# A statically scheduled attention + gated-FFN kernel: wider spacing of score visits, new latencies in the scheduler, and a different split of buffer memory

## The chip, the cores and the metric

One core of one Trainium2 chip. The metric is the device time of one execution in microseconds (us), median of several executions. The profile's span is from the first to the last instruction, here about 1.8 us shorter than the time. TensorE is called PE, VectorE DVE, ScalarE ACT, GpSimd POOL, SyncE SP, as in the profile.

## The reference, cut to what matters

```python
B, S, D, F = 1, 2048, 576, 4608;  H = 32; Dh = 18; W = 256          # bf16
xn = layernorm(x)
q, k, v = split_heads(xn @ wqkv)                                      # 32 heads of 18
p  = softmax(where(0 <= i - j < W, q k^T * Dh**-0.5, -1e9))           # sliding window
s  = concat_heads(p @ v) @ wo
g  = silu((sigmoid(xn @ w_gate) * (xn @ w_up)) @ w_down)
out = x + s * g
```

## The kernel before

The program is one long list of operations (`Op`), each with an engine, an estimated duration and what it depends on. A list scheduler plays the operations through in estimated time and fixes the order on each engine; then code is emitted with semaphore waits. So the constants below don't change what is computed. They change the order.

The sequence is cut into four chunks of 512 rows. For a chunk PE computes the projections of Q, K and V, the scores (in "score visits", short groups of matmuls whose PSUM result ScalarE's exp reads: 5 for each of 8 head groups in 4 chunks, 160 in all), the PV products (16 blocks), the output projection, 36 gate/up tiles and the down projections. Attention of the next chunk runs between the gate/up tiles of this one.

A matmul has 64 rows. Two of them, on the upper and the lower half of the array, run at the same time as a pair (in this kernel's trace 3793 such starts, of some 4150 pairs, are 3 to 4 ns apart). A gate/up tile is 5 pairs, then 4 pairs with the halves swapped. The second part adds to the PSUM banks of the first, so it waits for the first part's semaphore: a "turn" (with nothing in between, the second part starts about 228 ns later than it could). Other matmuls placed between the two parts hide that wait.

```python
NWS = 3            # gate/up weight buffers
NQD = 1            # staging buffers between the Q/K projection and the q/k slots
NFIN = 2           # also the number of tanh buffers of the output stage
NWARM = 36
SPACE_NS = 1100.0  # least distance of two score visits
...
# Pool.pick: when a PSUM unit is free again
free.append((max(now, max(r.end for r in h.rel) + 90.0), self.units.index(u), u))
...
# warm-up matmuls: fillers, taken while PE has nothing else, dropped at the first gate/up tile
w = op("PE", 432 if i < 9 else 216, f_warm, f"warm:{i}", deps=[z], prio=4, acq=None if i else h, odeps=[w])
...
# the output stage: tanh -> t; t *= y; t *= s_attn (the attention branch); x += t
th = op("ACT", act_ns(w), lambda e: f_th(e, 0, 2), f"fth:{nm}", deps=[f2, dt_], prio=0)
q1 = op("DVE", ..., f"fq1:{nm}", deps=[th, f2], prio=0)
q2 = op("DVE", ..., f"fq2:{nm}", deps=[q1, self.op_s[sb]], prio=2)
h.release(q1)                       # PSUM is free after q1 ...
self.r_th.release(st, q3)           # ... the tanh buffer only after the attention branch came
...
# schedule(): candidates of PE
st = max(free[e], ready_t[o.cidx])
if e == "PE" and o.name.startswith("sc"):
    st = max(st, last_sc + SPACE_NS)
...
k = (st + o.prio * self.PRIO_NS, o.cidx)
...
# schedule(): latency from one operation to its successor
lat = (250.0 if o.eng == "PE" and o in s_.deps else 20.0) if s_.eng == o.eng else (200.0 if o.eng == "PE" else 90.0)
if s_.eng == "PE" and o.eng != "PE":
    lat += 600.0 if o.lane is not None else 100.0
```

The softmax here doesn't subtract the row's maximum and nothing guards it: scores larger than these inputs give would overflow.

Of the kernel before, what the change touches and what calls it, by code (L numbers as in the profile page):

```python
# [8 lines left out]
D = 576  # L9
# [12 lines left out]
FG = 4  # L22
NFG = NFT // FG
WG = 2
NWS = 3
EPS = 1e-5
SM_SCALE = float(DH) ** -0.5

# [22 lines left out]
NXR = 2  # L51
NXN = 2
NST = 3
NQD = 1
NFIN = 2
NTAIL = 96
NWARM = 36
PARTS = (((0, 1), (1, 2), (2, 4)), ((0, 1), (1, 2), (2, 4)), ((0, 2), (2, 4)))
# [5 lines left out]
FLIP_ISSUE_NS = 1280.0  # L64
FLIP_SLACK_NS = 2700.0
SHARE_NS = 300.0
SPACE_NS = 1100.0
DMA_BYTES_PER_NS = 280.0
DMA_QUEUE_NS = 2400.0

# [59 lines left out]
class Pool:  # L130
# [11 lines left out]
    def pick(self, n, now, barred=()):  # L142
        free = []
        for u in self.units:
            if u in barred:
                continue
            h = self.last[u]
            if h is None:
                free.append((0.0, self.units.index(u), u))
            elif h.rel and all(r.idx >= 0 for r in h.rel):  # L150
                free.append((max(now, max(r.end for r in h.rel) + 90.0), self.units.index(u), u))
        if len(free) < n:
            return None
        free.sort()
        got = free[:n]
        return max(g[0] for g in got), sorted(g[2] for g in got)
# [70 lines left out]
class Builder:  # L227
# [38 lines left out]
    def alloc_memory(self):  # L266
        nc = self.nc
        bf16, f32 = dt.bfloat16, dt.float32
        cur = [(nc.sbuf_base + 63) // 64 * 64]
        top = nc.sbuf_top  # L270

        def size(shape, dtp):
            n = 1
            for s_ in shape[1:]:
                n *= s_
            return n * mybir.dt.size(dtp)

        def seq(name, shape, dtp=bf16, align=32):
            off = (cur[0] + align - 1) // align * align
            cur[0] = off + size(shape, dtp)  # L280
            assert cur[0] <= top, f"out of SBUF at {name}: {cur[0]} > {top}"
            return nc.alloc_sbuf_tensor_at(name, list(shape), dtp, offset=off), off

        self.xnT, _ = seq("xnT", [P, 2, KB, NT])
        self.wd_sb, _ = seq("wd_sb", [P, NFT, D])
        self.hT, _ = seq("hT", [P, NFT, NT])
        self.wgs, _ = seq("wgs", [P, NWS, KB - 1, 2, WG * P])
        self.wgr, _ = seq("wgr", [P, F])
        self.tring, _ = seq("tring", [P, 2, NT])
        self.v_aug, _ = seq("v_aug", [P, NVS * VSZ])  # L290
        self.qk, _ = seq("qk", [P, NQS, 2, NT])
        self.kprev, _ = seq("kprev", [P, NHG, NT // 2])
        self.kx, _ = seq("kx", [P, NKX, 12, 2, SW])
        self.expr, zex = seq("expr", [P, NEX, 2, NT])
        self.x0 = nc.alloc_sbuf_tensor_at("x0", [P, BPC, D], bf16, offset=zex)
        assert size([P, BPC, D], bf16) <= size([P, NEX, 2, NT], bf16)
        self.ot1, _ = seq("ot1", [P, 1, NT], f32)
        self.o2, _ = seq("o2", [P, 1, NT])
        self.o2T, _ = seq("o2T", [P, 2, NT])
        self.oT, _ = seq("oT", [P, KB, NT])  # L300
        self.s_attn, _ = seq("s_attn", [P, BPC, D])
        self.wqk, _ = seq("wqk", [P, KB - 1, 2, D])
        self.wqkr, _ = seq("wqkr", [P, D])
        self.wq4, _ = seq("wq4", [P, KB, 2, RD])
        self.wv_sb, _ = seq("wv_sb", [P, KB - 1, D])
        self.wvr, _ = seq("wvr", [P, D // 2])
        self.wo_sb, _ = seq("wo_sb", [P, KB - 1, D])
        self.wor, _ = seq("wor", [P, D // 2])
        self.qd, _ = seq("qd", [P, NQD, 2, NT])
        self.xr, _ = seq("xr", [P, NXR, D])  # L310
        self.xnr, _ = seq("xnr", [P, NXN, XW])
        self.xf, _ = seq("xf", [P, NFIN, D])
        self.thf, _ = seq("thf", [P, NFIN, D])
        self.ident, _ = seq("ident", [P, SW])
        self.mask, _ = seq("mask", [P, P])
        self.small, _ = seq("small", [P, 3 + 16 * NST], f32)
        sm = self.small
        self.neghalf, self.half = sm[:, 0:1], sm[:, 1:3]
        self.bnst = sm[:, 3:3 + 12 * NST].rearrange("p (s i c) -> p s i c", i=2, c=6)
        self.mv = sm[:, 3 + 12 * NST:3 + 14 * NST].rearrange("p (s c) -> p s c", c=2)  # L320
        self.veps = sm[:, 3 + 14 * NST:3 + 15 * NST].rearrange("p (s c) -> p s c", c=1)
        self.rstd = sm[:, 3 + 15 * NST:3 + 16 * NST].rearrange("p (s c) -> p s c", c=1)
        if self.verbose:
            print(f"SBUF used up to {cur[0]} of {top} ({top - cur[0]} free)")
        self.ps = nc.alloc_psum_tensor("ps", [P, 4096], f32)
        self.psb = self.ps.bitcast(bf16)
        last = {}
        self.pool_s = Pool("S", [0, 1], last)
        self.pool_f = Pool("F", [2, 3, 1], last)

    def build_graph(self):
# [8 lines left out]
        self.r_o2 = Ring(1, "o2")  # L340
        self.r_o2T = Ring(2, "o2T")
        self.r_w = Ring(NWS, "wgs")
        self.r_t = Ring(2, "tring")
        self.r_xf = Ring(NFIN, "xf")
        self.r_th = Ring(NFIN, "th")
        self.xnT_rel = [[] for _ in range(NC)]
        self.op_xnT = [[] for _ in range(NC)]
        self.op_v = {}
# [216 lines left out]
    def build_qk(self, c, gi):  # L565
# [13 lines left out]
        def rhs(r, t, k):  # L579
            t0 = t * n if gi == 4 else 0  # L580
            return self.xnT[r, xs, k, t0:t0 + n]
        pj = self.two("qk", f"{c}:{gi}", n, h, lhs, rhs, [self.op_xnT[c], self.op_wqk if gi < 4 else self.op_wqk4], n)
        self.xnT_rel[c].append(pj)

        def f_ev(eng):
# [5 lines left out]
        for u in range(H):  # L591
# [1 line left out]
            if lo >= hi:  # L593
                continue
            hg, p0, n_ = u // 4, 32 * (u % 4) + lo - DH * u, hi - lo
            if (c, hg) not in self.q_slot:
                self.q_slot[(c, hg)] = self.r_q.produce()
            qs, war = self.q_slot[(c, hg)]
            s0 = lo - gi * P
            if gi < 4:  # L600
# [226 lines left out]
    def build_ffn(self, c):  # L827
        op = self.op
        xs = c % 2
        x_in = self.xnT[:, xs, :, :]  # L830
        slots = {}
        wops = {}
        hm = {}
        if c == 0:
# [9 lines left out]
        def weights(wg):  # L844
            sw, dw = self.r_w.produce()
            pr = 1 + wg if c == 0 and wg < 4 else 3
            fc = slice(wg * WG * P, (wg + 1) * WG * P)
            ds = [self.load_nat(self.wgs[:, sw, :, i, :], w[:, fc], f"dma:w:{c}:{wg}", ("w", sw, i), pr, [dw])
                  for i, w in enumerate((self.wg, self.wu))]
            if c == 0:  # L850
                if wg % 2 == 0:
                    f8 = slice(wg * WG * P, (wg + 2) * WG * P)
                    self.op_wgr[wg] = self.load_rem(self.wgr[:, f8], (self.wg[:, f8], self.wu[:, f8]), f"dma:wgr:{wg}",
                                                    ("wgr", wg % NWS), pr, [dw])
                ds += self.op_wgr[wg - wg % 2]
            slots[wg] = sw
            wops[wg] = ds

# [10 lines left out]
        def gate_up(ft, h, half, acq, part=None, deps=()):  # L869
# [3 lines left out]
            xin = self.op_xnT[c][b0:b1]  # L873

            def lhs(r, t, k):
                return self.wgs[r, sw, k - 1, t, fc] if k else self.wgr[r, ft * P:(ft + 1) * P]

            def f(eng):
                return turn(eng, [bank(h, w)[:, t0:t0 + n] for w in range(2)], lhs, lambda r, t, k: x_in[r, k, t0:t0 + n], half)
# [31 lines left out]
        for ft in range(early, NFT):  # L911
            if ft % WG == 0 and ft // WG not in slots:
                weights(ft // WG)
            h = self.pool_f.hold()
            lo = gate_up(ft, h, 0, h)
            u = gate_up(ft, h, 1, None, None, [lo])
            tail(ft, h, u)
            if c == 0 and ft % FG == FG - 1:
                load_wd(ft // FG)
            if ft % WG == WG - 1:  # L920
                self.r_w.release(slots[ft // WG], u)
        self.xnT_rel[c].append(self.ffn_last)
        self.hm = hm

# [89 lines left out]
    def schedule(self):  # L1014
# [14 lines left out]
        while nsched < len(ops):  # L1029
            best = None  # L1030
            for e in ENGS:
# [4 lines left out]
                if e == "PE":  # L1036
                    for o in cand:
                        if o.acq is not None:
                            claims.setdefault(o.acq.pool.name, []).append((o.prio, o.cidx, ready_t[o.cidx]))
                bk = None  # L1040
                for o in cand:
                    st = max(free[e], ready_t[o.cidx])
                    if e == "PE" and o.name.startswith("sc"):
                        st = max(st, last_sc + SPACE_NS)
                    units = None
                    if o.acq is not None:
                        mine = o.acq.pool
# [9 lines left out]
                        units = got[1]  # L1057
                        if any((p_, c_) < (o.prio, o.cidx) and r_ <= st + 300.0 for p_, c_, r_ in claims[mine.name]):
                            continue
                    k = (st + o.prio * self.PRIO_NS, o.cidx)  # L1060
                    if bk is None or k < bk[0]:
                        bk = (k, o, st, units)
                if bk is not None and (best is None or (bk[2], ENGS.index(e)) < best[0]):
# [29 lines left out]
            prog[o.eng].append(o)  # L1093
            for s_ in o.succs:
                remaining[s_.cidx] -= 1
                lat = (250.0 if o.eng == "PE" and o in s_.deps else 20.0) if s_.eng == o.eng else (200.0 if o.eng == "PE" else 90.0)
                if s_.eng == "PE" and o.eng != "PE":
                    lat += 600.0 if o.lane is not None else 100.0
                ready_t[s_.cidx] = max(ready_t[s_.cidx], o.end + lat)
                if remaining[s_.cidx] == 0:  # L1100
                    enabled[s_.eng].append(s_)
# [120 lines left out]
```

## Time and profile before

| | before |
|---|---|
| time, median (range) | 567.83 us (566.67 to 567.88) |
| span of the profile | 565.9 us |
| PE busy | 558.6 us (99%) |
| first gate/up matmul starts | 9.27 us |
| PE not streaming, 36 us to the end | 8.4 us, of which 2.9 at PV blocks |

The page of the kernel before: busy times by engine, the chain of waits, and three of the costliest groups (busy us, mean ns of one, idle time before them).

```profile
span 565.9 us, 19089 instructions
PE 558.6 (99%) x8300; PEld 332.3 (59%) x8300; DVE 330.8 (58%) x793; ACT 267.8 (47%) x379; POOL 212.2 (37%) x358
...
PE 96%; DVE 2%; ACT 1%; issue 1%; DVEq 0%
...
L700 ACT ACTIVATE expr<-ps 128x1024 bf16<-128x1024 f32 (+2 forms) x160 | 156.0, 983 | 60.6 <-PE ps L100 60.1
...
L891 DVE SCALAR_TENSOR_TENSOR hT<-tring,ps 128x512 bf16<-128x512 bf16 x144 | 98.3, 684 | 76.8 <-ACT tring L888 74.4
L888 ACT ACTIVATE tring<-ps 128x512 bf16<-128x512 f32 x144 | 85.7, 596 | 119.6 <-PE ps L100 118.4
```

PE bounds the kernel, but "99% busy" hides stalls. In this trace a 512-column matmul is drawn 376 ns long, and the next pair starts after 216 ns. So lost time has to be read from starts. Pairs follow each other after 216 ns at 512 columns and 56 ns at 128 without a stall. "Not streaming" in this document is the sum, over the trace, of how much later than that the next matmul starts (a base of a few ns more or less shifts each sum by some tenths of a us).

A stall looks like this in the timeline of the kernel before (start us, us, engine, line, operation, out<-in; in brackets idle time and what ended it):

```profile
40.72 0.30 PE L100 MATMUL ps<-qk,kx 64*128 64x320 bf16 x2
40.85 1.89 PE L100 MATMUL ps<-xnT,wgs 64*128 64x512 bf16 x16
...
42.58 0.38 PE L100 MATMUL ps<-qk,kx 64*128 64x320 bf16 x4
42.61 1.49 DVE L891 SCALAR_TENSOR_TENSOR hT<-tring,ps 128x512 bf16<-128x512 bf16 x2
...
42.79 0.60 ACT L888 ACTIVATE tring<-ps 128x512 bf16<-128x512 f32 x1 [0.27 <-PE ps L100]
...
43.34 0.39 PE L100 MATMUL ps<-xnT,wgr 64*128 64x512 bf16 x2 [0.38 <-DVE hT L891]
```

The gate/up tile at 43.34 waits for the gate multiply on DVE (`hT`), which frees its PSUM banks; start to start it comes 541 ns too late. There are four such gaps of 489 to 585 ns (42.8, 47.7, 52.8, 259.0 us), five unfilled turns of about 228 ns, and a number of half-filled turns.

### The profile page before, as it was taken

The numbers are of one execution on the slowest core, as the hardware profiler recorded it, in microseconds if no ns is written. First come the engines' busy times: TensorE is split into PE (matmuls) and PEld (weight loads), VectorE is DVE, ScalarE is ACT, GpSimd is POOL, SyncE is SP. The second block draws the span as 40 slices with busy tenths as digits, with TensorE's granted clock in tenths as the row PEclk, the third lists the DMA queues.
The fourth block names the chain that finished last, engine by engine and source line by source line (L and its number), as shares of the span: only waits on it lengthen the run. The fifth ranks groups of instructions, "written<-read, shape, count | busy, mean of one in ns | idle before, by whom it ended". The sixth has DMA issues, their size and how long they took to land.

```text
span 565.9 us, 19089 instructions
## 1 busy us (share of the span) xinstructions
PE 558.6 (99%) x8300; PEld 332.3 (59%) x8300; DVE 330.8 (58%) x793; ACT 267.8 (47%) x379; POOL 212.2 (37%) x358
## 2 busy tenths in 40 slices
PE   8999999999999999999999999999999999999997
PEld 5554444577764455554777655544567754444786
DVE  5476868857596777468476836867752133333133
ACT  2256457445554973574386356659721022332111
POOL 5643646662492735336474434817210000000000
PEclk9999999999999999999999999999999999999999
DMA  8869876723124543233620133544430025443010
GB/s 245 238 200 217 242 205 181 218 66 67 54 57 130 153 122 100 64 114 105 105 61 16 55 94 102 147 124 132 123 88 22 23 62 168 134 128 114 1 44 24
DMA packets 109003, 64.27 MB, mean 114 GB/s; under 512 B 17612, under 2 KB 107052, under 8 KB 108920
## 3 DMA queue, kind: packets, MB, share of 16 engines
q1 hardware_dynamic: 101496, 57.13, 36.5%
q0 software_dynamic: 7424, 5.92, 4.0%
q8 instruction: 65, 1.06, 0.8%
q14 instruction: 18, 0.15, 0.1%
HBM read 51.61 MB, written 2.36 MB: 95 GB/s over the span
## 4 chain that ended last, share of the span: by engine, by line
PE 96%; DVE 2%; ACT 1%; issue 1%; DVEq 0%
PE ps L100 93%; PE ps L750 3%; DVE hT L891 1%; ACT tring L888 0%; ACT expr L700 0%; DVE ot L768 0%; DVE s_attn L994 0%; DVE expr L713 0%; DVE thf L999 0%; DVE kx L665 0%; ACT xnT L526 0%; DVE o2T L776 0%; DVE o L772 0%; DVE xf L1004 0%; PE ps L549 0%
## 5 line engine op out<-in xcount | busy, mean ns | idle before, releaser
L100 PE MATMUL ps<-xnT,wgs 64*128 64x512 bf16 (+2 forms) x2384 | 290.2, 369 | 0.5
L700 ACT ACTIVATE expr<-ps 128x1024 bf16<-128x1024 f32 (+2 forms) x160 | 156.0, 983 | 60.6 <-PE ps L100 60.1
L100 PEld LDWEIGHTS ps<-xnT,wgs 64*128 64x128 bf16 x2384 | 109.2, 94 | 117.0 <-PE ps L100 4.4
L100 PE MATMUL ps<-wd_sb,hT 64*128 64x288 bf16 (+2 forms) x2448 | 153.6, 276 | 0.0
L891 DVE SCALAR_TENSOR_TENSOR hT<-tring,ps 128x512 bf16<-128x512 bf16 x144 | 98.3, 684 | 76.8 <-ACT tring L888 74.4
L888 ACT ACTIVATE tring<-ps 128x512 bf16<-128x512 f32 x144 | 85.7, 596 | 119.6 <-PE ps L100 118.4
L100 PEld LDWEIGHTS ps<-wd_sb,hT 64*128 64x128 bf16 x2448 | 112.8, 94 | 27.9
L256 POOL DMA_DIRECT2D qk<-qd x160 | 81.8, 519 | 69.6 <-DVE qd L587 45.0
L713 DVE TENSOR_TENSOR expr<-expr,mask 128x256 bf16<-128x256 bf16 (+2 forms) x232 | 64.9, 305 | 53.4 <-ACT expr L700 52.7
L665 POOL TENSOR_SCALAR kx<-kprev,small 128x256 bf16<-128x256 bf16 x64 | 63.2, 995 | 60.4 <-PE ps L100 59.9
L100 PE MATMUL ps<-qk,kx 64*128 64x320 bf16 (+4 forms) x736 | 59.6, 251 | 0.0
L100 PE MATMUL ps<-xnT,wgr 64*128 64x512 bf16 (+2 forms) x298 | 55.6, 369 | 1.7 <-DVE hT L891 1.5
L100 PEld LDWEIGHTS ps<-qk,kx 64*128 64x128 bf16 x736 | 32.3, 94 | 27.8 <-ACT expr L700 0.7
L256 POOL DMA_DIRECT2D oT<-o2T x72 | 36.9, 519 | 30.1 <-DVE o2T L776 16.9
L984 ACT ACTIVATE thf<-ps 128x576 bf16<-128x576 f32 (+3 forms) x22 | 11.4, 519 | 61.1 <-PE ps L100 60.6
L100 PE MATMUL ps<-xnT,wqk 64*128 64x512 bf16 x256 | 32.6, 376 | 0.0
L768 DVE STREAM_TRANSPOSE ot<-ps 128x512 f32<-128x512 f32 x32 | 22.4, 700 | 15.8 <-PE ps L750 15.7
L669 POOL COPY kprev<-qk 128x256 bf16<-128x256 bf16 x32 | 13.6, 427 | 40.1 <-DVE kx L665 38.8
L665 DVE TENSOR_SCALAR kx<-qk,small 128x512 bf16<-128x512 bf16 x64 | 23.4, 390 | 7.3 <-PE ps L100 6.2
L987 DVE SCALAR_TENSOR_TENSOR thf<-thf,ps 128x576 bf16<-128x576 bf16 x12 | 9.0, 750 | 31.1 <-ACT thf L984 30.9
L100 PEld LDWEIGHTS ps<-xnT,wgr 64*128 64x128 bf16 x298 | 14.7, 94 | 16.7 <-DVE hT L891 3.9
L647 ACT ACTIVATE v_aug<-ps 64x288 bf16<-64x288 f32 x32 | 13.1, 409 | 23.1 <-PE ps L100 22.6
(64 smaller groups left out, 324.7 us busy)
## 6 DMA issues: line engine op xcount, KB each, us to landing
wgs<-in_B_w_gate_dram SPq DMA_DIRECT2D x72, 256.0 KB, 3.1
wgs<-in_B_w_up_dram SPq DMA_DIRECT2D x72, 256.0 KB, 3.6
wd_sb<-in_B_w_down_dram SPq DMA_DIRECT2D x9, 576.0 KB, 4.7
qk<-qd POOLq DMA_DIRECT2D x100, 36.0 KB, 2.0
xf<-in_A_x_dram SPq DMA_DIRECT2D x16, 144.0 KB, 2.2
out_dram<-xf SPq DMA_DIRECT2D x16, 144.0 KB, 1.8
xr<-in_A_x_dram SPq DMA_DIRECT2D x6, 288.0 KB, 4.1
wqk<-in_A_wqkv_dram SPq DMA_DIRECT2D x2, 576.0 KB, 6.4
```

The source lines that it names most:

```text
L100: res = eng.matmul(outs[i], lhs(ROWS[t], i), rhs(ROWS[t], i), start=start, stop=stop, tile_position=(64 * t, 0))
L256: o = self.op(eng, DMA_ISSUE_NS[eng], lambda e: e.dma_start(dst, src), name, deps, prio, nbytes=nbytes)
L647: return eng.activation(dst, src, ACTF.Copy)
L665: return e.tensor_scalar(self.kx[:, sx, pos:pos + n_ // SW, t, :], src.rearrange("p (s k) -> p s k", k=SW), self.half[:, t:t + 1], None, A ...
L669: self.op_kp[hg] = op("POOL", 420, lambda e: e.tensor_copy(self.kprev[:, hg, :], self.qk[:, qs, 1, NT // 2:NT]), f"kp:{c}:{hg}", deps=[kxo ...
L700: return eng.activation(self.expr[:, se, :, lo * SW:NT], self.both(h, NT)[:, :, lo * SW:NT], ACTF.Exp, scale=SM_SCALE)
L713: return eng.tensor_tensor(e_, e_, m_, ALU.mult)
L750: res = eng.matmul(outs[i][p0:p0 + VH, cols], self.v_aug[ROWS[i], o:o + VH], self.expr[ROWS[i], se, t, cols], start=n == 0, stop=n == len( ...
L768: return e.transpose(self.ot1[:, p1, :], self.halves(hp, NT)[i])
L888: th = op("ACT", act_ns(NT), lambda e: e.activation(self.tring[:, st, :], bank(h, 0), ACTF.Tanh, scale=0.5), f"th:{c}:{ft}", deps=[pg, dt_ ...
L891: mu = op("DVE", dve_ns(NT), lambda e: e.scalar_tensor_tensor(self.hT[:, ft, :], self.tring[:, st, :], 1.0, bank(h, 1), ALU.add, ALU.mult) ...
L984: return e.activation(v2(t)[:, a:b, :], y2()[:, a:b, :], ACTF.Tanh, scale=0.25)
```

## The change

The intent: spread the score visits (1700 instead of 1100 ns) and let one be placed early where PE would otherwise idle, so that visits fill turn gaps; give the scheduler other latencies, two of them nearer to the trace (from the end of a DVE instruction to the matmul that waits for it 58 ns: new 60, old 90 to 190; a turn about 228 ns: new 235, old 250; for the others, 210 ns from PE and 690 ns from a DMA, it was not shown); and use SBUF differently. The first 64 rows ("remainder rows") of all gate/up weights, resident so far, go through a ring of two and are reloaded in each chunk. The room goes to a fourth gate/up buffer, a second staging buffer and four tanh buffers. A Q/K projection now waits for its q slot (the buffer that its result goes to) before it starts.

```diff
-NWS = 3
+NWS = 4
+NWR = 2
-NQD = 1
+NQD = 2
+NTH = 4
-SPACE_NS = 1100.0
+TURN_WAIT_NS = 235.0
+PE_OUT_NS = 210.0
+PE_IN_NS = 60.0
+DMA_PE_NS = 690.0
+FILL_NS = 100.0
+SPACE_NS = 1700.0
@@ Pool.pick
-                free.append((max(now, max(r.end for r in h.rel) + 90.0), ...
+                free.append((max(now, max(r.end for r in h.rel) + PE_IN_NS), ...
@@ alloc_memory
-        self.wgr, _ = seq("wgr", [P, F])
+        self.wgr, _ = seq("wgr", [P, NWR, 2 * WG * P])
-        self.thf, _ = seq("thf", [P, NFIN, D])
+        self.thf, _ = seq("thf", [P, NTH, D])
@@ build_qk (the slots were produced after the projection before)
+        wars = [self.q_slot[(c, hg)][1] for hg in range(NHG) if (c, hg) in self.q_slot]
-        pj = self.two("qk", ..., [self.op_xnT[c], self.op_wqk if gi < 4 else self.op_wqk4], n)
+        pj = self.two("qk", ..., [self.op_xnT[c], self.op_wqk if gi < 4 else self.op_wqk4, wars], n)
@@ weights()
-            if c == 0:
-                if wg % 2 == 0: ... load_rem(self.wgr[:, f8], ..., [dw])
+            if wg % 2 == 0:
+                sr, dr = self.r_wr.produce()
+                ... load_rem(self.wgr[:, sr, :], ..., [dr])
@@ schedule()
+                            due = last_sc + SPACE_NS if o.name.startswith("sc") else 0.0
-                            claims...append((o.prio, o.cidx, ready_t[o.cidx]))
+                            claims...append((o.prio, o.cidx, max(ready_t[o.cidx], due)))
-                        st = max(st, last_sc + SPACE_NS)
+                        early = min(max(0.0, last_sc + SPACE_NS - st), FILL_NS)
-                    k = (st + o.prio * self.PRIO_NS, o.cidx)
+                    k = (st + early + o.prio * self.PRIO_NS, o.cidx)
@@ schedule(), latency to a successor
-                lat = (250.0 if PE to PE else 20.0) ... 200.0 / 90.0, + 600.0 or 100.0 towards PE
+                same engine: TURN_WAIT_NS if PE to PE else 0.0; from a DMA: DMA_PE_NS to PE else 90.0;
+                else PE_OUT_NS from PE, PE_IN_NS to PE, 50.0
```

(The lines under the last `@@` paraphrase the code; "..." and all that is not shown are cuts.)

More of the change, by code (lines that the diff above doesn't have):

```diff
@@ L150, in pick @@
             elif h.rel and all(r.idx >= 0 for r in h.rel):
-                free.append((max(now, max(r.end for r in h.rel) + 90.0), self.units.index(u), u))
+                free.append((max(now, max(r.end for r in h.rel) + PE_IN_NS), self.units.index(u), u))
         if len(free) < n:
@@ L342, in build_graph @@
         self.r_w = Ring(NWS, "wgs")
+        self.r_wr = Ring(NWR, "wgr")
         self.r_t = Ring(2, "tring")
         self.r_xf = Ring(NFIN, "xf")
-        self.r_th = Ring(NFIN, "th")
+        self.r_th = Ring(NTH, "th")
         self.xnT_rel = [[] for _ in range(NC)]
@@ L581, in rhs @@
             return self.xnT[r, xs, k, t0:t0 + n]
-        pj = self.two("qk", f"{c}:{gi}", n, h, lhs, rhs, [self.op_xnT[c], self.op_wqk if gi < 4 else self.op_wqk4], n)
+        for u in range(gi * P // DH, ((gi + 1) * P - 1) // DH + 1):
+            if u < H and (c, u // 4) not in self.q_slot:
+                self.q_slot[(c, u // 4)] = self.r_q.produce()
+        wars = [self.q_slot[(c, hg)][1] for hg in range(NHG) if (c, hg) in self.q_slot]
+        pj = self.two("qk", f"{c}:{gi}", n, h, lhs, rhs, [self.op_xnT[c], self.op_wqk if gi < 4 else self.op_wqk4, wars], n)
         self.xnT_rel[c].append(pj)
@@ L595, in build_qk @@
             hg, p0, n_ = u // 4, 32 * (u % 4) + lo - DH * u, hi - lo
-            if (c, hg) not in self.q_slot:
-                self.q_slot[(c, hg)] = self.r_q.produce()
             qs, war = self.q_slot[(c, hg)]
@@ L831, in build_ffn @@
         slots = {}
+        rslots = {}
         wops = {}
@@ L849, in weights @@
                   for i, w in enumerate((self.wg, self.wu))]
-            if c == 0:
-                if wg % 2 == 0:
-                    f8 = slice(wg * WG * P, (wg + 2) * WG * P)
-                    self.op_wgr[wg] = self.load_rem(self.wgr[:, f8], (self.wg[:, f8], self.wu[:, f8]), f"dma:wgr:{wg}",
-                                                    ("wgr", wg % NWS), pr, [dw])
-                ds += self.op_wgr[wg - wg % 2]
+            if wg % 2 == 0:
+                f8 = slice(wg * WG * P, (wg + 2) * WG * P)
+                sr, dr = self.r_wr.produce()
+                rslots[wg // 2] = sr
+                self.op_wgr[wg] = self.load_rem(self.wgr[:, sr, :], (self.wg[:, f8], self.wu[:, f8]), f"dma:wgr:{c}:{wg}",
+                                                ("wgr", sr), pr, [dr])
+            ds += self.op_wgr[wg - wg % 2]
             slots[wg] = sw
@@ L875, in lhs @@
             def lhs(r, t, k):
-                return self.wgs[r, sw, k - 1, t, fc] if k else self.wgr[r, ft * P:(ft + 1) * P]
+                return self.wgs[r, sw, k - 1, t, fc] if k else self.wgr[r, rslots[ft // (2 * WG)], ft % (2 * WG) * P:(ft % (2 * WG) + 1) * P]
             def f(eng):
@@ L921, in build_ffn @@
                 self.r_w.release(slots[ft // WG], u)
+            if ft % (2 * WG) == 2 * WG - 1:
+                self.r_wr.release(rslots[ft // (2 * WG)], u)
         self.xnT_rel[c].append(self.ffn_last)
@@ L1038, in schedule @@
                         if o.acq is not None:
-                            claims.setdefault(o.acq.pool.name, []).append((o.prio, o.cidx, ready_t[o.cidx]))
+                            due = last_sc + SPACE_NS if o.name.startswith("sc") else 0.0
+                            claims.setdefault(o.acq.pool.name, []).append((o.prio, o.cidx, max(ready_t[o.cidx], due)))
                 bk = None
@@ L1042, in schedule @@
                     st = max(free[e], ready_t[o.cidx])
+                    early = 0.0
                     if e == "PE" and o.name.startswith("sc"):
-                        st = max(st, last_sc + SPACE_NS)
+                        early = min(max(0.0, last_sc + SPACE_NS - st), FILL_NS)
                     units = None
@@ L1095, in schedule @@
                 remaining[s_.cidx] -= 1
-                lat = (250.0 if o.eng == "PE" and o in s_.deps else 20.0) if s_.eng == o.eng else (200.0 if o.eng == "PE" else 90.0)
-                if s_.eng == "PE" and o.eng != "PE":
-                    lat += 600.0 if o.lane is not None else 100.0
+                if s_.eng == o.eng:
+                    lat = TURN_WAIT_NS if o.eng == "PE" and o in s_.deps else 0.0
+                elif o.lane is not None:
+                    lat = DMA_PE_NS if s_.eng == "PE" else 90.0
+                else:
+                    lat = PE_OUT_NS if o.eng == "PE" else PE_IN_NS if s_.eng == "PE" else 50.0
                 ready_t[s_.cidx] = max(ready_t[s_.cidx], o.end + lat)
```

## The prediction

> **What bounds the kernel now.** TensorE. The page has PE busy 558.6 of 565.9 us (99%), the chain of waits is 96% PE, the granted clock 1.00. A busy PE may still stall: [...] a 512-column matmul is drawn 376 ns long, but the next pair starts after 216 ns. So I counted from start to start in the timeline. Then PE streams for 549.3 us. The rest:
> - before the first matmul 1.0 us; warm-up at half rate 2.35; after the last matmul 4.1, and 1.9 from span to reported time;
> - 16 PV blocks: 90 ns before and 93 ns after each, 2.9 us. [...] only PV has 19-column tiles, and its blocks show these gaps;
> - 10 to 36 us: 0.8 us;
> - 36 to 440 us: about 5.5 us. Four are score visit -> gate/up gaps of 489 to 585 ns, waiting for VectorE's gate multiply to free PSUM (two visits too near each other hold banks and ScalarE); five are 228 ns gate/up turns, where the second half waits for the first half's semaphore and nothing fills the gap; the rest are 64 to 232 ns, mostly turns half filled by a short visit;
> - 440 us to the last matmul: nothing.
>
> **What the change does.** No matmul, activation or vector instruction is removed or added.
> - Score visits: 1700 instead of 1100 ns apart, but early where the alternative starts over 100 ns later, so that they stand in turn gaps. Today 89 of 159 intervals are 1.0 to 1.4 us, while one exp (0.98 us) and one tanh (0.60 us) need 1.58 us of ScalarE. 160 visits need 272 us; today they stretch over 377.
> - Latencies in the static schedule match the trace: VectorE's end to PE's start is 58 ns (new 60, old 90 to 190), turns 228 to 235 (new 235).
> - Q/K projection waits for its q slot before it starts, so it can't hold PSUM and staging; two staging buffers.
> - Fourth gate/up buffer, four tanh buffers: PE waits on no weights worth naming after the start, so about 0 directly.
> - Remainder rows in a ring: reloaded in the three later chunks, 54 more DMA issues (SP spends about 0.5 us each, 27 us over 430) and about 3.5 MB beside 64. DMA share there is 0.2 to 0.45; hidden. In 36 to 60 us, where DMA is 0.90 busy, bytes stay the same.
>
> **On the critical path.** Only the 5.5 us between 36 and 440 us. [...] The floor is about 567.8 - 6.3 = 561.5 us. I expect 60 to 75% of the 5.5 us back: about 4 us.
>
> **Prediction: 563.8 us**, 8 in 10 within 561.3 to 567.0. Faster by over 2%: 0.01; within: 0.97; slower: 0.02.
>
> **Signs.** Right: the 500 ns gaps at 42, 47, 52 and 258 us vanish; PV gaps stay; visits mostly 1.6 to 2.0 us apart; the last visit no earlier than now (413 us); ScalarE's and VectorE's busy times unchanged. Wrong: PE waits on a weight queue; output projection of the last chunk slips beyond 530 us; idle PE in 440 to 530 us.
>
> **What would make it wrong.** Visits spread so far that the last chunk's attention delays the end (slower); [...] a start-up that the new order also shortens (faster, under 2 us).

549.3 us of streaming and 1.0 + 2.35 + 4.1 + 1.9 + 2.9 + 0.8 + 5.5 us of the rest make 567.85 us, and the floor takes off 5.5 and 0.8. "Half rate" means warm-up pairs that start 401 to 427 ns apart instead of 216 (11 intervals in the kernel before).

## The result, and the profile after

565.38 us median (564.75 to 566.35, 4 runs) against 567.83 us. The ratio is 0.9963, 95% interval 0.9943 to 0.9983. Ratios here are the mean time of one kernel's fast runs over that of the other's of the same rounds, so not quite the ratio of the medians. The gain is 2.5 us where 4 were predicted; the time lies inside the predicted range.

The page of the kernel after, the same lines:

```profile
span 563.4 us, 19190 instructions
PE 557.3 (99%) x8306; PEld 345.6 (61%) x8306; DVE 340.7 (60%) x793; ACT 269.3 (48%) x379; POOL 209.3 (37%) x358
...
PE 96%; DVE 2%; DMA 1%; issue 0%; ACT 0%; DVEq 0%
...
L710 ACT ACTIVATE expr<-ps 128x1024 bf16<-128x1024 f32 (+2 forms) x160 | 156.8, 980 | 110.2 <-PE ps L107 109.6
...
L903 DVE SCALAR_TENSOR_TENSOR hT<-tring,ps 128x512 bf16<-128x512 bf16 x144 | 98.1, 683 | 57.0 <-ACT tring L900 53.2
L900 ACT ACTIVATE tring<-ps 128x512 bf16<-128x512 f32 x144 | 85.9, 597 | 88.9 <-PE ps L107 86.5
```

The work is the same; the chain of waits has a new member, a DMA with 1%. Where the span's 2.6 us come from, counted from the starts of matmuls:

| us | before | after | difference |
|---|---|---|---|
| first gate/up matmul starts | 9.27 | 10.21 | +0.94 |
| PE not streaming, 10 to 36 us | 0.77 | 0.55 | -0.22 |
| from 36 us on, at PV blocks | 2.91 | 2.99 | +0.08 |
| from 36 us on, elsewhere | 5.53 | 2.78 | -2.75 |
| after the last matmul | 3.83 | 3.65 | -0.18 |
| not attributed | | | -0.44 |
| span | 565.94 | 563.37 | -2.57 |

The row "elsewhere" has two parts. From 36 to 440 us, the stretch that the prediction named, 5.53 us became 2.05; behind 440 us, where the kernel before had none, 0.72 us are new.

All four old 500 ns gaps are gone. But new waits came, above all two. In the timeline of the kernel after, two gate/up tiles end between two visits, and the next tile waits for a Q/K eviction on DVE (`qd`, 1.19 us), which ends 60 ns before that tile starts; the gate multiply comes only after it. The tile is 516 ns late:

```profile
66.67 1.19 DVE L599 CAST qd<-ps 128x1024 bf16<-128x1024 f32 x1
...
67.23 0.33 PE L107 MATMUL ps<-qk,kx 64*128 64x64 bf16 x4
...
67.78 1.27 DVE L903 SCALAR_TENSOR_TENSOR hT<-tring,ps 128x512 bf16<-128x512 bf16 x2
...
67.92 0.39 PE L107 MATMUL ps<-xnT,wgr 64*128 64x512 bf16 x2 [0.35 <-DVE qd L599]
```

And the chain of waits of the kernel after in the stretch from 90 to 120 us (start us, us, what) goes through the load of the last down weights, for which PE waited 474 ns. (The wait differs between executions: the profiles of `hard_spacing` and `warm_again` below, with the same order on PE, do not have it.)

```profile
98.84 0.69 DVE hT L903
99.52 0.03 DVE small L499
99.55 6.13 DMA wd_sb<-in_B_w_down_dram
105.68 0.14 issue
105.82 12.42 PE ps L107 x198
```

The start is later as well. The timelines of PE, before and then after: warm-up matmuls (`hT`), the transposes of the first two row blocks, and the first gate/up matmul (`xnT,wgr`).

```profile
1.28 5.70 PE L100 MATMUL ps<-hT 64*128 64x512 bf16 x30 [1.28 <-DVE hT L423]
...
6.96 1.67 PE L100 MATMUL ps<-hT 64*128 64x512 bf16 x14
...
8.62 0.81 PE L100 MATMUL ps<-hT 64*128 64x512 bf16 x6
9.27 0.22 PE L100 MATMUL ps<-xnT,wgr 64*128 64x128 bf16 x2
```

```profile
1.28 6.21 PE L107 MATMUL ps<-hT 64*128 64x512 bf16 x32 [1.28 <-DVE hT L431]
...
7.47 1.67 PE L107 MATMUL ps<-hT 64*128 64x512 bf16 x14
...
9.13 1.24 PE L107 MATMUL ps<-hT 64*128 64x512 bf16 x10
10.21 0.22 PE L107 MATMUL ps<-xnT,wgr 64*128 64x128 bf16 x2
```

Before, 50 warm-up matmuls (25 pairs) run first; after, 56 (28 pairs). The texts of expectations below count time from the first computing instruction, 0.31 us later than these timelines, so their 8.96 and 9.90 us are the 9.27 and 10.21 us here. The prediction made the same slip: its 1.0 us before the first matmul and 4.1 us after the last are 1.3 and 3.8 us of the span, with the same sum.

### The profile page after: what moved, and what is told of

It reads as the page before. It is cut to its first block, busy times and chain, and to the rows that moved or that the text cites. A ratio compares the mean times of both kernels' runs of the same rounds, so it can differ in the third digit from the quotient of the medians.

```text
span 563.4 us, 19190 instructions
## 1 busy us (share of the span) xinstructions
PE 557.3 (99%) x8306; PEld 345.6 (61%) x8306; DVE 340.7 (60%) x793; ACT 269.3 (48%) x379; POOL 209.3 (37%) x358
## 3 DMA queue, kind: packets, MB, share of 16 engines
q0 software_dynamic: 7424, 5.92, 3.9%
## 4 chain that ended last, share of the span: by engine, by line
PE 96%; DVE 2%; DMA 1%; issue 0%; ACT 0%; DVEq 0%
PE ps L107 92%; PE ps L760 3%; DMA wd_sb<-in_B_w_down_dram 1%; DVE ot L778 0%; DVE o2T L786 0%; DVE o L782 0%; DVE hT L903 0%; DVE qd L599 0%; DVE s_attn L1008 0%; DVE thf L1013 0%; DVE ot L781 0%; ACT xnT L534 0%; DVE xf L1018 0%; ACT tring L900 0%; PE ps L557 0%
## 5 line engine op out<-in xcount | busy, mean ns | idle before, releaser
L107 PE MATMUL ps<-xnT,wgs 64*128 64x512 bf16 (+2 forms) x2384 | 286.3, 369 | 0.1
L107 PEld LDWEIGHTS ps<-xnT,wgs 64*128 64x128 bf16 x2384 | 116.2, 94 | 111.3 <-PE ps L107 0.9
L107 PE MATMUL ps<-wd_sb,hT 64*128 64x288 bf16 (+2 forms) x2448 | 155.4, 276 | 0.3 <-DMA wd_sb<-in_B_w_down_dram 0.3
L107 PEld LDWEIGHTS ps<-wd_sb,hT 64*128 64x128 bf16 x2448 | 117.1, 94 | 25.5 <-issue 0.6
L675 POOL TENSOR_SCALAR kx<-kprev,small 128x256 bf16<-128x256 bf16 x64 | 60.9, 960 | 129.0 <-PE ps L107 128.7
L107 PEld LDWEIGHTS ps<-qk,kx 64*128 64x128 bf16 x736 | 33.5, 94 | 26.0 <-DVE ot L778 1.3
L599 DVE CAST qd<-ps 128x1024 bf16<-128x1024 f32 (+1 forms) x20 | 21.9, 1094 | 3.0 <-PE ps L107 3.0
```

The costliest lines, as they stand in the source:

```text
L107: res = eng.matmul(outs[i], lhs(ROWS[t], i), rhs(ROWS[t], i), start=start, stop=stop, tile_position=(64 * t, 0))
L599: return eng.tensor_copy(dst, self.both(h, n))
L675: return e.tensor_scalar(self.kx[:, sx, pos:pos + n_ // SW, t, :], src.rearrange("p (s k) -> p s k", k=SW), self.half[:, t:t + 1], None, A ...
```

## The experiments

The theories. A: the scheduling rules bring the gain, and buffers are worth about nothing, as predicted. B: the buffers bring it. C: the new rules need the buffers. D: the start lost time to extra warm-up. Times of different calls come from different chips, so they are compared through their ratio to the kernel before, which ran beside each (medians 567.7 to 568.0 us).

### Each half of the change alone

`storage_only`: the changed kernel with the old scheduling rules and constants (edit in words).

```diff
-SPACE_NS = 1700.0   (and filling rule, due times in claims, all new latencies)
+SPACE_NS = 1100.0   (and the old rules and latencies, as before)
```

> Only the storage half of the change (four gate/up buffers, remainder ring, two staging and four tanh buffers, q slots taken before the projection); the scheduling rules are those of before. Theory A (the rules bring the gain, storage nothing by itself): 567 to 568.5 us, ratio to before 0.998 to 1.002, and gaps of about 500 ns behind close score visits as before. Theory B (more buffers bring the gain): 565.4 us, ratio 0.996.

Measured: 568.74 us, ratio 1.0011 (0.9994 to 1.0027). Not streaming from 36 us on: 7.99 us against 8.44 before; gaps of 368 to 590 ns behind visits are there in number, here one in the timeline of this run, a visit and the gate/up tile that waits for the gate multiply (`hT`) after it:

```profile
72.63 0.69 DVE L903 SCALAR_TENSOR_TENSOR hT<-tring,ps 128x512 bf16<-128x512 bf16 x1
...
72.77 0.27 PE L107 MATMUL ps<-qk,kx 64*128 64x256 bf16 x2
...
73.37 0.39 PE L107 MATMUL ps<-xnT,wgr 64*128 64x512 bf16 x2 [0.33 <-DVE hT L903]
```

B falls. The reloading of the remainder rows (in the changed kernel 54 more DMA issues, and 67.8 MB moved instead of 64.3) is in this kernel too and shows no net cost in the time. It was not run alone, though, and the down weights take longer from issue to landing here and in the changed kernel (median 5.8 and 6.4 us, before 4.7), so a share of it in the new wait for them is not excluded.

`rules_only`: the new rules with the old numbers of buffers.

```diff
-NWS = 4
+NWS = 3
-NQD = 2
+NQD = 1
-NTH = 4
+NTH = 2
```

> Only the scheduling half: spacing, filling and the new latencies, with three gate/up buffers, one staging and two tanh buffers (the remainder ring stays). Theory A as the prediction had it (buffers are worth about 0): 565 to 566 us, like the whole change. Theory C (the new rules need the buffers, because wider visits put the output projection behind the start of the down projection, 401 against 381 us in the changed kernel's third chunk, so finished tiles wait for it): 568 us or more, slower than before, with PE waits on the final multiplies in the down projections.

Measured: 579.15 us, ratio 1.0193 (1.0165 to 1.0221). A falls in its second half, C stands: the rules alone are 1.9% slower than no change, the buffers alone change nothing, and both together are 0.4% faster. The largest wait, in the timeline of this run, is the one for the down weights, 2.7 us:

```profile
105.06 1.63 PE L107 MATMUL ps<-wd_sb,hT 64*128 64x288 bf16 x24
...
109.23 2.10 PE L107 MATMUL ps<-wd_sb,hT 64*128 64x288 bf16 x16 [2.54 <-DMA wd_sb<-in_B_w_down_dram]
```

The waits on final multiplies that the text expected are not this one; the next runs separate the buffers. The Q/K projection's wait for its q slot is in both halves: without it the scheduler found no order at all under the new rules, so that part couldn't be tried by itself and stays open.

### One kind of buffer at a time

`tanh_two`:

```diff
-NTH = 4
+NTH = 2
```

> The changed kernel with two output tanh buffers instead of four, nothing else edited (the static order follows from it). Theory A: 565.4 us, no difference. Theory C: 2 us or more slower, 567.5 us and up, the loss lying in the down projections of the chunks whose output projection comes after their start (240 to 290 us and 380 to 440 us).

Measured: 570.26 us, ratio 1.0050 (1.0033 to 1.0067); not streaming from 36 us on 10.07 us (5.77 in the changed kernel). The size agrees with C. The place does not: the loss lies not at 240 to 290 or 380 to 440 us but at 146 to 159 us, between the first and the second chunk. The timelines of PE there, first of the changed kernel, then of `tanh_two`:

```profile
145.92 0.66 PE L107 MATMUL ps<-wv_sb,xnT 64*128 64x288 bf16 x8
146.41 0.38 PE L107 MATMUL ps<-xnT,wgr 64*128 64x512 bf16 x2
146.63 1.03 PE L107 MATMUL ps<-xnT,wgs 64*128 64x512 bf16 x8
147.49 0.66 PE L107 MATMUL ps<-wv_sb,xnT 64*128 64x288 bf16 x8
147.98 1.03 PE L107 MATMUL ps<-xnT,wgs 64*128 64x512 bf16 x8
```

```profile
145.97 1.39 PE L107 MATMUL ps<-wv_sb,xnT 64*128 64x288 bf16 x16
148.26 0.30 PE L107 MATMUL ps<-wvr,xnT 64*128 64x288 bf16 x2 [0.90 <-DVE qd L599]
148.39 1.38 PE L107 MATMUL ps<-wv_sb,xnT 64*128 64x288 bf16 x16
149.61 0.29 PE L107 MATMUL ps<-wvr,xnT 64*128 64x288 bf16 x2
149.74 1.39 PE L107 MATMUL ps<-wv_sb,xnT 64*128 64x288 bf16 x16
```

In the changed kernel gate/up tiles (`xnT,wgs`) of the next chunk stand between the V projections (`wv_sb`) and fill each other's turns. With two tanh buffers no gate/up tile runs between 146 and 159 us; V and output projections run alone, their turns of 220 to 230 ns open. The code gives the reason, and the tanh of the third finished tile (`thf`) fits it. In the timelines of ACT, first of the changed kernel, then of `tanh_two`, it starts at 138.72 and at 157.10 us:

```profile
138.72 0.65 ACT L998 ACTIVATE thf<-ps 128x576 bf16<-128x576 f32 x1
```

```profile
157.10 0.65 ACT L998 ACTIVATE thf<-ps 128x576 bf16<-128x576 f32 x1
```

The reason: wider visits put the output projection at 154 to 162 us, behind the end of the down projection (145 us; before, it came at 136 to 142 us, ahead of it). A finished tile keeps its tanh buffer until the attention branch has come; with two buffers the other finished tiles then keep their PSUM, which the next gate/up tiles need.

`staging_one` and `weights_three`:

```diff
-NQD = 2
+NQD = 1
```

> The changed kernel with one Q/K staging buffer instead of two. Prediction's view (buffers about 0): 565.4 us. Theory C (the new rules lean on the buffers): 568 us or more, idle PE from 36 us on 8 us or more.

Measured: 568.62 us, ratio 1.0019 (1.0004 to 1.0033), 9.05 us not streaming from 36 us on. As C expected.

```diff
-NWS = 4
+NWS = 3
```

> The changed kernel with three gate/up weight buffers instead of four. Prediction's view (the trace shows no PE wait on weights): 565.4 us. Theory C: 567 us or more, idle PE from 36 us on 7.5 us or more, with waits on weight loads named.

Measured: 567.15 us, ratio 1.0000 (0.9979 to 1.0020), 7.98 us not streaming from 36 us on. As C expected in size; a wait of 1.0 us for the down weights at 104.8 us is the largest. So the three kinds of buffers, together worth nothing under the old order, each carry some tenths of a per cent under the new one. A rival is left: each of these edits also shuffles the whole order, and `short_and_early` below, which only moves a load, lost 0.8 to 1.4 us of stalls. The three lost 2.2 to 4.3 us, so the shuffle alone is unlikely, but how much of each is the buffer itself was not tested.

### The rules one by one

`close_visits`:

```diff
-SPACE_NS = 1700.0
+SPACE_NS = 1100.0
```

> The changed kernel with the score visits 1100 ns apart again, all else new (filling rule, latencies, buffers). Theory A (the spacing brings the gain): 567.5 us or more, the gaps of about 500 ns behind close visits back, idle between 36 and 440 us some 2 to 4 us larger than in the changed kernel. Rival (the latencies bring it): 565.4 us. The first gate/up matmul stays at 9.9 us.

Measured: 578.37 us, ratio 1.0174 (1.0153 to 1.0196). In the expected direction, but far more than expected: 19.3 us not streaming from 36 us on, of which 12.0 between 60 and 145 us. Four visits pile up with little between them, held by the exps of others (PE stood idle for 0.64, 0.91 and 0.78 us between 107 and 111 us, each time with the exp named). The windows of this run (us; PE, PEld, DVE, ACT, POOL busy; granted clock; DMA share; GB/s):

```profile
100.00:107.00 7.00, 7.00 (x102) 4.54 (x98) 4.96 (x14) 2.92 (x4) 4.40 (x8) 1.00 0.68 170
107.00:112.00 5.00, 1.64 (x22) 0.57 (x16) 1.73 (x7) 3.42 (x4) 2.06 (x3) 0.87 0.96 258
112.00:121.00 9.00, 7.88 (x118) 4.90 (x120) 6.50 (x16) 1.04 (x3) 2.59 (x6) 0.50 0.17 53
121.00:130.00 9.00, 9.00 (x157) 7.08 (x154) 4.25 (x16) 5.60 (x7) 3.29 (x5) 1.00 0.30 69
```

From 110.7 us, still within the pile-up, PE ran 10.2 us at half clock (column before the DMA share: 0.50). Most of the loss is thus a pile-up at one place and its aftermath. Outside 60 to 145 us this run loses 7.3 us against 3.8 in the changed kernel, 3.5 us more, as theory A expected. The worth of the spacing alone can't be read from this run, as buffers and latencies are the new ones.

`old_latencies` is a better reading of it (edit in words):

```diff
-TURN_WAIT_NS, PE_OUT_NS, PE_IN_NS, DMA_PE_NS and 50.0 / 0.0 in the successor's latency
+the old expression (250/20, 200/90, + 600 or 100 towards PE), 90.0 in Pool.pick
```

> The changed kernel with the schedule's old latencies, spacing, filling and buffers new. Theory A (spacing is enough): 564.5 us, as the old latencies bring the start back to 8.96 us (25 warm-up pairs) and the gaps stay few. Rival (the latencies carry part of the gain): 567 us or more in spite of the earlier start, with more unfilled turns of about 228 ns.

Measured: 565.29 us, ratio 0.9954 (0.9936 to 0.9971). It is not slower than the whole change (0.9963), so the rival falls; nor did it reach 564.5. From 36 us on it loses 6.61 us instead of 5.77, but its warm-up is the old one of 25 pairs. The new latencies bring some 0.8 us in the middle (up to 1.5, by the other profiles of the new order below: 5.51, 5.72 and 5.13 us) and by the times give it back, at the start. Between this kernel and `storage_only` (1.0011) there is only the spacing with its filling rule: 0.57%, about 3.2 us (1.9 to 4.6 with both intervals taken together). By the times that is the whole gain. The two profiles show less of it: 1.4 us fewer stalls from 36 us on (7.99 and 6.61), while 1.0 us of the difference of their spans is an earlier start from an earlier full clock (see "The start"). The profile of `storage_only` was the fastest of its executions (566.89 us, median 568.74), which may be why. So the direction is shown; how much of the 3.2 us is the spacing, between 1.4 and all, is not.

`hard_spacing`:

```diff
-                        early = min(max(0.0, last_sc + SPACE_NS - st), FILL_NS)
+                        st = max(st, last_sc + SPACE_NS)
```

> The changed kernel with 1700 ns as a hard limit: a visit is never placed early, so it can't be drawn forward to fill a turn. If filling by early visits matters, more turns of 228 ns stand open and it is 0.5 to 1.5 us slower, 566 to 567 us. If the spacing alone does it, 565.4 us within 0.5, and nearly the same order of work.

Measured: 566.5 us, ratio 0.9978 (0.9958 to 0.9998). By the time this looks like the first case, but the two programs' instruction orders were compared: PE, ACT, POOL and SP have the same order, and DVE differs at one place. From 36 us on the two lose 5.51 and 5.77 us. So the filling rule did nothing here, and this run is in effect a repetition of the changed kernel: the 1.1 us between 565.4 and 566.5 are what such repetitions differ by. Any verdict here on less than a microsecond rests on trace positions, not on times.

### The start

`warm_short`:

```diff
-432 if i < 9 else 216
+432 if i < 13 else 216
```

More warm-up pairs are taken as slow, so fewer fit: 24. The order of everything else on PE is the same.

> The changed kernel with 24 warm-up pairs instead of 28; the order of everything else is the same. Theory D (the change lost 0.94 us at the start, the first gate/up matmul at 9.90 us instead of 8.96, because its new latencies let three more warm-up pairs in ahead of the real work): first gate/up matmul at 9.0 to 9.1 us and the time 0.8 to 0.9 us below the changed kernel, 564.5 us. Rival (the later start is the input's arrival, 0.1 us later in that profile, and the same with any warm-up): 565.4 us.

Measured: 563.80 us, ratio 0.9931 (0.9919 to 0.9944). First gate/up matmul at 8.22 us on the text's clock. Faster than expected, and the profiles of all runs say why the reading of 0.94 us was itself in part chance. Warm-up pairs start 427 ns apart at first and 216 ns apart later; in the kernel before this changes where the trace's record of the granted clock begins, at 1.00, so there PE went from half to full clock. In the 13 fast profiles that moment lies between 3.6 and 6.7 us on the text's clock, which this paragraph and the table keep, and at another time in nearly every run. For the seven fast profiles with 28 warm-up pairs the first gate/up matmul follows that moment:

| full clock from (us) | 3.62 | 3.96 | 4.56 | 5.92 | 6.20 | 6.23 | 6.67 |
|---|---|---|---|---|---|---|---|
| first gate/up (us) | 8.60 | 8.77 | 9.07 | 9.74 | 9.88 | 9.90 | 10.11 |

The slope is 0.5. The kernel before got full clock at 5.63 us; at that moment 28 pairs would give 9.60 us (an estimate from the slope) and 25 pairs gave 8.96. So three more pairs cost 0.64 us, and 0.30 us of the 0.94 were a later clock. 25 pairs with full clock from 3.61 us (`old_latencies`) gave 7.96 us, 1.0 us earlier than the same 25 in the kernel before.

`after_again` and `warm_again`, the changed kernel and the same with 24 pairs, side by side:

> The changed kernel itself once more, to be compared with the short warm-up on one chip, and with the hard-spacing run, whose order on TensorE is the same: 565 to 566.5 us, the runs spread over about 1.5 us, as the number of warm-up pairs at half rate (8 to 13 in the runs of kernels with 28 pairs) moves the first gate/up matmul between 9.1 and 10.1 us. Idle PE from 36 us on 5.5 to 5.8 us.

> The changed kernel with 24 warm-up pairs, once more beside the changed kernel. Theory D: 0.9 to 1.7 us below the changed kernel of the same rounds, and a smaller spread (0.8 us), as the start then waits for the layer norm on VectorE and not for the clock. Rival (the earlier difference was the chip): within 0.4 us of the changed kernel.

Measured: the changed kernel 563.63 to 565.92 us in five fast runs, mean 564.89, ratio 0.9952 (0.9939 to 0.9965); with 24 pairs 563.58 to 564.65 us, mean 563.86, ratio 0.9934 (0.9922 to 0.9946). The difference is 1.03 us, as theory D expected, but the intervals overlap (0.9939 to 0.9946). The profiled execution of `after_again` (727 us, clock 0.752 from 4.1 us to the end) is left out, so its stall count can't be given. Theory D's reason for the small spread is not settled: in the profile of `warm_again` the start did follow the clock (full from 6.13 us, first gate/up 8.98 us); in that of `warm_short` it waited for the layer norm on DVE (0.3 us).

### A try for more

`short_and_early`:

```diff
-432 if i < 9 else 216
+432 if i < 13 else 216
-deps=[hm[fg * FG + 2]], prio=6))
+deps=[hm[max(2, fg * FG - 2)]], prio=6))
```

> The changed kernel with 24 warm-up pairs and the down weights asked for one group (about 8 us) earlier. The wait for them at the first down projection (474 ns in the changed kernel, 587 ns with the short warm-up) should vanish: 563.2 us, 0.5 to 0.6 below the short warm-up alone (563.8). If the earlier loads crowd the gate/up loads out, 564 us or more.

Measured: 564.81 us, ratio 0.9942 (0.9927 to 0.9957). The wait for down weights did vanish, but it is no gain over the shorter warm-up alone (0.9931 and 0.9934). Moving a load moved the whole order: a 288 ns and a 365 ns wait that name DMA semaphores, and waits of 265 to 364 ns around Q/K projections and visits, are new; from 36 us on 6.54 us are lost against 5.72 (`warm_short`) and 5.13 (`warm_again`, in which the down weights happened to be in time). The best version is the changed kernel with 24 warm-up pairs, 563.7 to 563.8 us.

## Why the prediction was right or wrong

- **Time and class: right.** 565.38 us lies in 561.3 to 567.0, and within 2%. The share that was open to the change was read well: apart from the start (below) nothing outside the stalls moved much, since no work was added or removed. The range was also wide: it held every gain from 0.8 to 6.5 us. PV gaps stayed (2.91 and 2.99 us).
- **"60 to 75% of the 5.5 us back": right for its stretch, and not the gain.** From 36 to 440 us 3.48 of 5.53 us came back, 63% (61 to 72% in four profiles of this order on PE). The four named gaps did vanish; a new order brings new waits, among them 516 ns behind a Q/K eviction and 474 ns for the down weights.
- **The missing term: "440 us to the last matmul: nothing".** Work that moved behind 440 us brought 0.72 us of new stalls (302 ns at 510.6 us and 220 ns at 518.6 us are the largest), so that over the whole run 2.75 of 5.53 us came back, 50%. The prediction named idle PE there as a sign of being wrong, but put no cost on it. Counting removable gaps gives the ceiling, not the gain.
- **"Only the 5.5 us between 36 and 440 us": the start moved too.** The first gate/up matmul came 0.94 us later, 0.64 of it from three warm-up pairs that the new latencies let in. The prediction had thought only of a shorter start. With this and the missing term, 3.5 us of removed stalls became a gain of 2.5.
- **Buffers "about 0 directly": true and misleading.** Alone they are worth nothing (1.0011). Under the new rules, going back on tanh buffers (1.0050), staging (1.0019) or weights (1.0000) each costs the whole gain or more, by the times (with the rival above). That they pay for what wider visits delay is seen for the tanh buffers (157.10 against 138.72 us) and argued for the others.
- **"So that they stand in turn gaps": shown wrong as a rule.** The filling rule changed no order on PE; the spacing did it, with the buffers.
- **Latencies: by the times they brought about as much as they cost** (565.29 us without them, 565.38 with).
- **Signs.** The last visit moved from 410 us (413 in the prediction) to 503 us and the last chunk's output projection to 520 to 525 us, inside the limit of 530. Visits are not mostly 1.6 to 2.0 us apart: 49 of 159 intervals are, 83 are 2.0 to 2.5 us. ACT's busy time stayed (267.8 and 269.3 us), DVE's rose from 330.8 to 340.7: 4.5 us of it are longer instructions, the rest is less overlap between them in the trace; why wasn't followed up. Two of the "wrong" signs appeared in small: the wait for a weight load, and 1.2 us lost at 440 to 530 us, about half of it the three PV blocks that moved there.
- **The ring: not contradicted.** 3.5 MB more, no net cost in `storage_only`; it was not run alone.

## What to carry to other kernels

In a statically ordered kernel, count stalls from start to start on the bounding engine: that gives the ceiling of any reordering, and about half of it was reached here, because each new order makes its own waits, also where there were none. Buffers that are worthless under one order can be what the next one stands on, so try halves of a change before calling one of them useless. When a change of constants moves the middle, look at the start too: there filler work took back a quarter of what the middle gained, and PE's full clock came at another moment in nearly every run (3.6 to 6.7 us), which makes that hard to see in times.

## What the traces showed of the clock and of waits

- Full clock came 2.6 to 5.7 us after the first matmul in 13 fast profiles; over the seven with 28 warm-up pairs the first real work moved by half as much.
- The clock halved for 3.4 us when a single wait of 2.7 us (`rules_only`) had lasted 2.4 us, and for 10.2 us after three late starts of 0.8 to 1.1 us in a row (`close_visits`; PE was busy for 1.64 of the 5 us from 107 to 112 us, so it did not stand still for the whole time).
- One execution of this single-core program (`after_again`) ran at 0.752 from 4.1 us to its end, 727 us. Why was not shown.
- In the kernel before, PE lost 90 ns before and 93 ns after each of the 16 PV blocks. Why was not shown.
- In the kernel before, a part of a gate/up tile that waited for the one just before it started 228 to 232 ns later than it could (seven times); after the end of a DVE instruction that it waited for, a matmul started 57 to 58 ns later (the four gaps of about 500 ns).
